# Windowed attention and a multiplicative feed-forward layer on one core: engine orders taken from a list schedule, row sums from added blocks, w_out loaded in halves

## The chip, the core and the metric

The kernel runs on one core of a Trainium2 chip. A core has five engines, each with an instruction stream of its own: TensorE (PE in the profile; PEld are its weight loads), VectorE (DVE), ScalarE (ACT), GpSimd (POOL) and SyncE (SP). They meet only through semaphores. Data lies in on-chip SBUF; TensorE writes its products to PSUM, a small accumulator memory. Loads and stores are DMA transfers issued by an engine's queue. Within an engine the instructions run in their written order, so an instruction that waits holds all that stand behind it.

The metric is the device time of one execution, in microseconds (us), as a median over runs.

## The reference

Attention over 4 batches, 8 heads, 768 positions and head size 64; a query sees the first four positions (the sinks) and the last 128. Its output goes, without a nonlinearity, through a feed-forward layer.

```python
    scores = scale * np.matmul(q, k.transpose(0, 1, 3, 2))
    keep = is_sink | in_window          # n_sink = 4, window = 128
    scores = np.where(keep, scores, -1000000000.0)
    a = np.exp(scores - max); a = a / (sum + 1e-09)
    attn = np.matmul(a, v)              # (4, 8, 768, 64)
    x = attn.transpose(0, 2, 1, 3).reshape(3072, 512)
    a = x @ w1                          # (512, 1024)
    b = x @ w2
    h = a * b @ w3                      # (1024, 1024)
    out = h @ w_out                     # (1024, 512)
```

Inputs are float32; the kernel casts them to bfloat16 in the loads and accumulates in float32.

## The kernel before, in words

**Fold.** As w3 and w_out are applied one after the other, the kernel first computes their product `w3o`. For each of the eight row blocks i of w3, `fold_w3(i)` transposes eight 128 x 128 blocks on TensorE (L249) and VectorE copies them out (L251); `fold_mm(i)` multiplies them by w_out in eight accumulating products of 512 columns (L257) and ScalarE copies the result to `w3o` (L259).

**Attention.** Per batch, k and q are transposed in three steps t of 256 positions (`transposes`, L154, copied by VectorE, L156). A unit is a pair of heads r (four) at a step t (three), so there are twelve a batch. `scores` computes the scores of a unit, keys on partitions (L191); ScalarE takes the exponential (L195, `ex`), VectorE multiplies by the mask (L198, `am`). At t = 0 there are three blocks of 128 x 128 per head, later four: for each of the two query blocks, the key block before it and its own, each masked to a triangle. `values` (L218) accumulates in one PSUM tile `av`, in column half 0 the products with v and in half 1 the row sums, which are products of the same `am` with a matrix of ones. The sinks have their own scores (`sink_scores`, L175, exponential L178) and values (`sink_values`, L163). ScalarE then forms the reciprocal of the sums as exp(-ln) (L223, L224), and VectorE multiplies (L225) into `xT`, the layer's input, transposed. The keys' and values' buffers are doubled or tripled over batches; `av` has one PSUM buffer, `sc` two, and all other products share three (`mm`).

**Layer.** `gate(b, c, dt)` makes one 128-row block dt of a and b for 384 tokens c of batch b: four products for `pa` (L233), a ScalarE copy (L236), four for `pb` (L239), and VectorE's multiplication (L241). There are 64 of these. `project(b, m)` makes 128 tokens of output from eight products of 512 columns (L265), a copy (L268) and a store by SP (L270). There are 24.

**What sets the order.** Loads are issued by GpSimd in one queue: w3's blocks 0 and 1, w_out, w3's blocks 2 to 4, then 5 to 7; after the selects that build masks, batch 0's k, q and v in blocks of 128 rows; w1 and w2 in halves; then the other batches. TensorE's order is written by hand: `attention(b)` steps through the units, and `fill(upto)` puts in the next piece of a list `dense` as a position advances through given spans. The list holds the fold, then each batch's gates and projections:

```python
    dense = [(0.6, fold_w3, (0,)), (0.6, fold_w3, (1,))]
    for i in range(KFF):
        if i + 2 < KFF:
            dense.append((0.45, fold_w3, (i + 2,)))
        dense.append((1.75, fold_mm, (i,)))
    ...
    spans = ((7.0, 17.6), (24.0, 49.2), (50.0, 80.0), (81.0, 110.0))
```

The transpose of w3 block 2 thus comes ahead of the first product with w_out, and batch 0's attention is spread over the rest of the fold. The framework orders ScalarE's and VectorE's instructions.

Of the kernel before, what the change touches and what calls it, by code (L numbers as in the profile page):

```python
# [21 lines left out]
def kernel(  # L22
# [81 lines left out]
    def load_w3(i0, n):  # L104
# [43 lines left out]
    def transposes(b, t):  # L148

        for src, dst in ((kN[b], kT[b]), (qN[b], qT[b])):  # L150
            tp = ps_mm.tile([P, NP, 2, P], BF16, tag="mm", name="tp")
            for r in range(NP):
                for i in range(2):
                    nc.tensor.transpose(tp[:, r, i, :], src[:, 2 * t + i, r * P:(r + 1) * P],  # L154
                                        ident[:])
            nc.vector.tensor_copy(dst[:, :, t * 256:(t + 1) * 256],  # L156
                                  tp[:].rearrange("p r i m -> p r (i m)"))

    def sink_values(b):

        vp = ps_mm.tile([P, H, D], FP32, tag="mm", name="vp")
        for h in range(H):
            nc.tensor.matmul(vp[:, h, :], sel[:, h, :], vN[b][:, 0, h * D:(h + 1) * D],  # L163
                             start=(h == 0), stop=(h == H - 1))
        nc.scalar.copy(vs[b][:], vp[:])
        for e in range(2):
            hp = slice(64 * e, 64 * e + 64)
            kk = ksbd[b][hp, 4 * e:4 * e + 640].rearrange("p (r x) -> p r x", x=160)
            nc.vector.tensor_copy(kk[:, :, 0:4], kT[b][hp, :, 0:4])

    def sink_scores(b, t):

        sp = ps_mm.tile([P, 256], FP32, tag="mm", name="sp")
        for r in range(NP):
            nc.tensor.matmul(sp[:], ksbd[b][:, r * P:(r + 1) * P],  # L175
                             qT[b][:, r, t * 256:(t + 1) * 256],
                             start=(r == 0), stop=(r == NP - 1))
        nc.scalar.activation(es[b][:, (t - 1) * 256:t * 256], sp[:], ACTF.Exp, scale=scale)  # L178


    def segments(t):
        segs = [] if t == 0 else [(2 * t - 1, 2 * t, P, 0)]
        return segs + [(2 * t, 2 * t, 2 * P, P), (2 * t + 1, 2 * t + 1, P, 3 * P)]

    def scores(b, r, t):
        c0 = P if t == 0 else 0
        sc = ps_sc.tile([P, 2, 512], FP32, tag="sc", name="sc")
        for i, (kb, qb, n, c) in enumerate(segments(t)):
            for e in range(2):
# [3 lines left out]
                                 start=True, stop=True)  # L193
        ex = work.tile([P, 2, 512], BF16, tag="ex", name="ex")
        nc.scalar.activation(ex[:, :, c0:], sc[:, :, c0:], ACTF.Exp, scale=scale)  # L195
        am = work.tile([P, 2, 512], BF16, tag="am", name="am")
        mk = maskt[:, min(t, 1):min(t, 1) + 1, c0:].to_broadcast([P, 2, 512 - c0])
        nc.vector.tensor_mul(am[:, :, c0:], ex[:, :, c0:], mk)  # L198
        return am

    def values(b, r, t, am):
# [3 lines left out]
        for kb, o, n, c in segs:  # L205
            for e in range(2):
                todo.append((e, 0, o, n, vN[b][:, kb, (2 * r + e) * D:(2 * r + e + 1) * D], am[:, e, c:c + n]))
            for e in range(2):
                todo.append((e, 1, o, n, ones[:], am[:, e, c:c + n]))
        if t > 0:  # L210
            sq = es[b][:, (t - 1) * 256:t * 256]
# [5 lines left out]
        for i, (e, y, o, n, lhs, rhs) in enumerate(todo):  # L217
# [3 lines left out]
            first[e] = False  # L221
        rec = work.tile([P, 256], FP32, tag="rec", name="rec")
        nc.scalar.activation(rec[:], av[:, 1, :], ACTF.Ln)  # L223
        nc.scalar.activation(rec[:], rec[:], ACTF.Exp, scale=-1.0)  # L224
        nc.vector.tensor_mul(xT[b][:, r, t * 256:(t + 1) * 256], av[:, 0, :], rec[:])  # L225

    def gate(b, c, dt):

        tk = slice(c * TOK, (c + 1) * TOK)
        d = slice(dt * P, (dt + 1) * P)  # L230
        pa = ps_mm.tile([P, TOK], FP32, tag="mm", name="pa")
        for kk in range(NP):
            nc.tensor.matmul(pa[:], w1_sb[:, kk, d], xT[b][:, kk, tk],  # L233
                             start=(kk == 0), stop=(kk == NP - 1))
        a_sb = work.tile([P, TOK], FP32, tag="a_sb", name="a_sb")
        nc.scalar.copy(a_sb[:], pa[:])  # L236
        pb = ps_mm.tile([P, TOK], FP32, tag="mm", name="pb")
        for kk in range(NP):
# [116 lines left out]
```

## Time and profile before

| what | us |
|---|---|
| median of three runs | 244.03 (243.27 to 245.24) |
| the profiled execution | 243.1 |
| its span, first to last instruction | 241.4 |
| TensorE busy | 214.9 |
| ScalarE busy | 132.7 |
| VectorE busy | 111.7 |

The profile is of one execution. Its page gives each engine's busy time, the span in 40 slices of about 6 us, the chain of work that ended last, and the costliest groups of instructions. The views of the trace behind it list instructions in order of time (the start, the duration, engine, line and operation, in brackets the idle time before it and what ended that), groups by shape, and who waited for whom. Matmuls are pipelined and their ends are modelled: successive ones overlap in these rows, so what a task takes of TensorE is read from one start to the next.

### The profile page before, as it was taken

The page shows a single profiled execution, that of the slowest core. Times are in us where ns is not written, and L with a number is a line of the kernel's source. Part 1 is how long each engine was busy: PE and PEld are TensorE (multiplying, and loading weights), DVE is VectorE, ACT ScalarE, POOL GpSimd, SP SyncE. Part 2 cuts the span into 40 slices and gives each one's busy share as a digit, 9 for nine tenths or more (in the row PEclk, how much of TensorE's full clock was granted, in tenths as well). Part 3 has the DMA queues.
Part 4 walks back from the last instruction along what each step waited for, and adds up shares of the span by engine and source line. Part 5 has one row for each costly group of instructions (what it writes and reads, how often), then busy time and mean ns, then how long its engine had stood idle before and what let it go on. Part 6 is the DMA issues. An engine that isn't in the chain of part 4 may idle for free.

```text
span 241.4 us, 4863 instructions
## 1 busy us (share of the span) xinstructions
PE 214.9 (89%) x1984; PEld 123.0 (51%) x1984; DVE 111.7 (46%) x211; ACT 132.7 (55%) x253; POOL 73.3 (30%) x90
## 2 busy tenths in 40 slices
PE   0329979687999999979999999999999999999994
PEld 0224656344656564446656654465565544566541
DVE  7202666542467664315656653157575531234300
ACT  2001576775365877744577777546766775333231
POOL 8946985499998098000000000000000000000000
PEclk9999999999999999999999999999999999999999
DMA  5999999999999999921000002220000022200033
GB/s 82 179 212 165 157 166 208 177 157 155 155 156 155 66 72 168 153 81 52 3 0 1 4 0 90 94 82 0 3 0 3 0 82 95 87 1 3 0 130 130
DMA packets 82582, 21.28 MB, mean 88 GB/s; under 512 B 75392, under 2 KB 78464, under 8 KB 82560
## 3 DMA queue, kind: packets, MB, share of 16 engines
q0 software_dynamic: 79104, 14.69, 74.5%
q1 hardware_dynamic: 3456, 6.29, 7.0%
q8 instruction: 15, 0.25, 0.4%
q14 instruction: 7, 0.06, 0.1%
HBM read 29.36 MB, written 6.29 MB: 148 GB/s over the span
## 4 chain that ended last, share of the span: by engine, by line
PE 85%; DMA 5%; ACT 4%; DVE 3%; issue 1%; POOL 1%; ACTq 0%; POOLq 0%
PE pa L233 19%; PE po L265 18%; PE pb L239 17%; PE av L218 13%; PE pw L257 7%; DMA w_sb<-in_moe_w_dram 5%; PE sc L191 5%; PE tp L154 4%; PE sp L175 1%; DVE xT_106 L225 1%; ACT rec L224 1%; ACT rec L223 1%; ACT ex L195 1%; ACT w3o L259 1%; DVE kT_102 L156 1%
## 5 line engine op out<-in xcount | busy, mean ns | idle before, releaser
L195 ACT ACTIVATE ex<-sc 128x1024 bf16<-128x1024 f32 (+1 forms) x48 | 45.3, 947 | 14.6 <-PE sc L191 14.6
L198 DVE TENSOR_TENSOR am<-ex,maskt 128x1024 bf16<-128x1024 bf16 (+1 forms) x48 | 31.1, 647 | 25.9 <-ACT ex L195 25.6
L236 ACT COPY a_sb<-pa 128x384 f32<-128x384 f32 x64 | 30.6, 478 | 21.9 <-DVE ab_113 L241 9.8
L239 PEld LDWEIGHTS <-w_sb 128*128 128x128 bf16 x256 | 25.0, 98 | 16.6
L233 PEld LDWEIGHTS <-w_sb 128*128 128x128 bf16 x256 | 21.8, 98 | 16.5 <-issue 4.3
L223 ACT ACTIVATE rec<-av 128x256 f32<-128x256 f32 x48 | 18.4, 383 | 16.5 <-PE av L218 16.3
L268 ACT COPY o_sb<-po 128x512 f32<-128x512 f32 x24 | 14.1, 586 | 20.8 <-PE po L265 20.8
L218 PE MATMUL av<-am,ones 128*64 128x128 bf16 (+1 forms) x256 | 24.1, 239 | 0.0
L224 ACT ACTIVATE rec<-rec 128x256 f32<-128x256 f32 x48 | 20.0, 417 | 1.5
L259 ACT CAST w3o<-pw 128x512 bf16<-128x512 f32 x8 | 4.7, 586 | 25.9 <-PE pw L257 25.9
L257 PE MATMUL pw<-wo_sb,w3t 128*128 128x512 bf16 x64 | 16.2, 399 | 0.5 <-ACT w3o L259 0.5
L241 DVE TENSOR_TENSOR ab_113<-a_sb,pb 128x384 bf16<-128x384 f32 x16 | 8.9, 555 | 14.8 <-PE pb L239 14.8
L218 PEld LDWEIGHTS <-ones 128*64 128x64 bf16 x256 | 14.8, 109 | 0.0
L233 PE MATMUL pa<-xT_108,w_sb 128*128 128x384 bf16 x64 | 13.2, 328 | 0.0
L233 PE MATMUL pa<-xT_107,w_sb 128*128 128x384 bf16 x64 | 13.1, 328 | 0.0
L233 PE MATMUL pa<-xT_106,w_sb 128*128 128x384 bf16 x64 | 13.1, 328 | 0.0
L239 PE MATMUL pb<-xT_108,w_sb 128*128 128x384 bf16 x64 | 13.0, 326 | 0.0
L239 PE MATMUL pb<-xT_107,w_sb 128*128 128x384 bf16 x64 | 13.0, 326 | 0.0
L239 PE MATMUL pb<-xT_106,w_sb 128*128 128x384 bf16 x64 | 13.0, 326 | 0.0
L233 PE MATMUL pa<-xT_109,w_sb 128*128 128x384 bf16 x64 | 13.0, 326 | 0.0
L239 PE MATMUL pb<-xT_109,w_sb 128*128 128x384 bf16 x64 | 13.0, 326 | 0.0
L249 PEld LDWEIGHTS <-w_sb 128*128 128x128 bf16 x64 | 4.8, 115 | 15.4 <-DMA w_sb<-in_moe_w_dram 14.7
(147 smaller groups left out, 361.3 us busy)
## 6 DMA issues: line engine op xcount, KB each, us to landing
out_dram<-o_sb SPq DMA_DIRECT2D x24, 256.0 KB, 2.0
w_sb<-in_moe_w_dram POOLq DMA_DIRECT2D x5, 512.0 KB, 10.5
w_sb<-in_moe_w_dram POOLq DMA_DIRECT2D x2, 768.0 KB, 14.7
wo_sb<-in_moe_w_out_dram POOLq DMA_DIRECT2D x1, 1024.0 KB, 10.4
kN_90<-in_k_dram POOLq DMA_DIRECT2D x6, 128.0 KB, 8.5
qN_86<-in_q_dram POOLq DMA_DIRECT2D x6, 128.0 KB, 7.1
vN_94<-in_v_dram POOLq DMA_DIRECT2D x6, 128.0 KB, 7.0
kN_91<-in_k_dram POOLq DMA_DIRECT2D x6, 128.0 KB, 7.3
```

Of the source, the lines that this page charges most:

```text
L191: nc.tensor.matmul(sc[:, e, c:c + n], kT[b][hp, r, kb * P:(kb + 1) * P], qT[b][hp, r, qb * P:qb * P + n], start=True, stop=True)
L195: nc.scalar.activation(ex[:, :, c0:], sc[:, :, c0:], ACTF.Exp, scale=scale)
L198: nc.vector.tensor_mul(am[:, :, c0:], ex[:, :, c0:], mk)
L218: nc.tensor.matmul(av[64 * e:64 * e + 64, y, o:o + n], lhs, rhs, start=first[e], stop=(i >= len(todo) - 2), skip_group_check=True)
L223: nc.scalar.activation(rec[:], av[:, 1, :], ACTF.Ln)
L224: nc.scalar.activation(rec[:], rec[:], ACTF.Exp, scale=-1.0)
L233: nc.tensor.matmul(pa[:], w1_sb[:, kk, d], xT[b][:, kk, tk], start=(kk == 0), stop=(kk == NP - 1))
L236: nc.scalar.copy(a_sb[:], pa[:])
L239: nc.tensor.matmul(pb[:], w2_sb[:, kk, d], xT[b][:, kk, tk], start=(kk == 0), stop=(kk == NP - 1))
L257: nc.tensor.matmul(po[:], w3T[i][:, j, :], wo_sb[:, j, :], start=(j == 0), stop=(j == KFF - 1))
L265: nc.tensor.matmul(po[:], ab[b][:, kk, m * P:(m + 1) * P], w3o[:, kk, :], start=(kk == 0), stop=(kk == KFF - 1))
L268: nc.scalar.copy(o_sb[:], po[:])
```

## The change: what it does

It has three parts.

1. *Loads.* w3 comes in blocks 0; 1; 2 and 3; 4 and 5; 6 and 7, and w_out in two halves of its columns, the first behind w3's block 0, the second behind block 3. `fold_mm` is split by the same halves: sixteen tasks of eight products of 256 columns. The transposed block of w3 has five buffers for two.
2. *Row sums.* For t > 0 VectorE adds, for each query block, its two masked key blocks into a tile `cs` (256 columns a head); as their masks are complementary triangles, the values are the window's terms at each place of the query, folded onto 128 partitions. The product with ones then runs once, over `cs`.
3. *Order.* Each piece of work becomes a task with stages on TensorE, ScalarE or VectorE, written as a Python generator that yields after each stage. Tasks have a priority, tasks that must be done or started before, loads they need and a PSUM ring. While the program is built, a list scheduler plays the stages through with written durations, modelled landing times and handovers of 0.2 us, and issues the instructions in the order in which that model starts them, on all three engines. A gate is two tasks, one for each half.

The core of the diff:

```diff
     nc.scalar.preload_act_table_set("natural_log_exp_and_others")
-    load_w3(0, 2)
-    load_w(wo_sb, moe_w_out, 0, DM)
-    load_w3(2, 3)
-    load_w3(5, 3)
     nc.vector.memset(ident[:], 1.0)
+    load_w3(0, 1)
     nc.gpsimd.affine_select(ident[:], ident[:], compare_op=ALU.is_equal, fill=0.0,
                             base=0, pattern=[[1, P]], channel_multiplier=-1)
+    load_w(wo_sb, moe_w_out, 0, DM // 2)
+    load_w3(1, 1)
+    load_w3(2, 2)
+    load_w(wo_sb, moe_w_out, DM // 2, DM)
+    load_w3(4, 2)
+    load_w3(6, 2)
...
-        am = work.tile([P, 2, 512], BF16, tag="am", name="am")
+        yield
+        am = work.tile([P, 2, 512], BF16, tag="am", bufs=4, name="am")
         mk = maskt[:, min(t, 1):min(t, 1) + 1, c0:].to_broadcast([P, 2, 512 - c0])
         nc.vector.tensor_mul(am[:, :, c0:], ex[:, :, c0:], mk)
+        cs = None
+        if t > 0:
+            cs = work.tile([P, 2, 256], BF16, tag="cs", bufs=4, name="cs")
+            a4 = am[:].rearrange("p e (a c q) -> p (e a) c q", c=2, q=P)
+            nc.vector.tensor_add(cs[:].rearrange("p e (a q) -> p (e a) q", q=P),
+                                 a4[:, :, 0, :], a4[:, :, 1, :])
+        ams[b, r, t] = am, cs
+        yield
...
             for e in range(2):
-                todo.append((e, 1, o, n, ones[:], am[:, e, c:c + n]))
+                if t == 0:
+                    todo.append((e, 1, o, n, ones[:], am[:, e, c:c + n]))
         if t > 0:
+            for e in range(2):
+                todo.append((e, 1, 0, 256, ones[:], cs[:, e, :]))
...
+    def gate(b, c, dt, half):
         tk = slice(c * TOK, (c + 1) * TOK)
+        w_sb = w2_sb if half else w1_sb
+        pg = ps_mm.tile([P, TOK], FP32, tag="mm", name="pg")
         for kk in range(NP):
+            nc.tensor.matmul(pg[:], w_sb[:, kk, dt * P:(dt + 1) * P], xT[b][:, kk, tk],
                              start=(kk == 0), stop=(kk == NP - 1))
+        yield
+        if half:
+            nc.vector.tensor_mul(ab[b][:, dt, tk], gate_a.pop((b, c, dt))[:], pg[:])
+        else:
+            a_sb = work.tile([P, TOK], FP32, tag="a_sb", bufs=4, name="a_sb")
+            nc.scalar.copy(a_sb[:], pg[:])
+            gate_a[b, c, dt] = a_sb
+        yield
...
+    def fold_mm(i, n):
+        po = ps_mm.tile([P, DM // 2], FP32, tag="mm", name="pw")
+        cols = slice(n * DM // 2, (n + 1) * DM // 2)
         for j in range(KFF):
+            nc.tensor.matmul(po[:], w3T[i][:, j, :], wo_sb[:, j, cols],
                              start=(j == 0), stop=(j == KFF - 1))
+        yield
+        nc.scalar.copy(w3o[:, i, cols], po[:])
+        yield
...
+    for i in range(KFF):
+        task(("t3", i), 100 + i, fold_w3(i), [("pe", 0.5), ("dve", 0.65)], loads=[("w3", i)],
+             started=[("fm", i - 5, 1)] if i > 4 else [], ring="mm")
+        for n in range(2):
+            task(("fm", i, n), 100.5 + i + 3 * n, fold_mm(i, n), [("pe", 0.9), ("act", 0.42)],
+                 [("t3", i)], [("wo", n)], "mm")
...
+                task(("sc", b, r, t), 4, scores(b, r, t),
+                     [("pe", 0.27), ("act", 0.83), ("dve", 0.58)] if t == 0 else
+                     [("pe", 0.36), ("act", 1.05), ("dve", 1.05)], after, ring="sc",
...
+                task(("av", b, r, t), 3, values(b, r, t),
+                     [("pe", 0.42 if t == 0 else 0.68), ("act", 0.85), ("dve", 0.45)],
...
+                task(("g", b, c, dt, 0), pr + 0.5, gate(b, c, dt, 0), [("pe", 0.66), ("act", 0.5)],
+                     [("av", b, NP - 1, last_t)] + war, [("w1", n), ("w2", n)], "mm",
+                     [("g",) + gates[-2] + (1,)] if len(gates) > 1 else [])
+                task(("g", b, c, dt, 1), pr, gate(b, c, dt, 1), [("pe", 0.66), ("dve", 0.56)],
+                     [("g", b, c, dt, 0)], ring="mm", half=True)
...
+    HOP = 0.2
+    MARGIN = {"av": 0.5}
+    BACKLOG = 1.6
+    free = {"pe": 0.0, "act": 0.0, "dve": 0.0}
+    rings = {n: [[0.0] for _ in range(k)] for n, k in (("mm", 3), ("sc", 2), ("av", 1))}
...
+    def pe_pick():
...
+            est = max([free["pe"]] + [arrive[x] + HOP for x in k["loads"]])
+            if not k["half"]:
+                est = max([est] + [done[a] + HOP for a in k["after"]])
+            if k["ring"]:
+                if rings[k["ring"]][0][0] is None:
+                    continue
+                est = max(est, rings[k["ring"]][0][0] + HOP)
+            if est > free["pe"]:
+                est += MARGIN.get(kind, 0.0)
+            if kind == "sc":
+                busy = max(0.0, free["act"] - free["pe"]) + sum(q[2] for q in queue["act"])
+                est = max(est, free["pe"] + busy - BACKLOG)
+            wait = est - free["pe"]
+            key = (0.0 if wait < 0.05 else wait, k["prio"])
...
+    with tc.manual_schedule(engines={mybir.EngineType.PE, mybir.EngineType.Activation,
+                                     mybir.EngineType.DVE}):
+        while len(done) < len(tasks):
+            pe = pe_pick()
+            moves = [(pe[2], 0, "pe")] if pe else []
+            for e in ("act", "dve"):
+                at = [when(q) for q in queue[e] if when(q) is not None]
+                if at:
+                    moves.append((max(free[e], min(at)), 1, e))
+            start, _, e = min(moves)
```

A lower number is a higher priority: transposes 1, sink work 2, values 3, scores 4, the fold 100 to 111, gates of batch b from 1000 + 200 b, its projections from 1300 + 200 b. The first two steps of a batch's attention open the gates of its first 384 tokens, the third those of its last 384; before, all of a batch's gates came behind its attention.

More of the change, by code (lines that the diff above doesn't have):

```diff
@@ new lines, in when, with advance @@
+    def when(q):
+        at, _, _, k = q
+        if k["half"]:
+            return max(at, done[k["after"][0]] + HOP) if k["after"][0] in done else None
+        return at
+    def advance(k, at):
+        i = k["stage"]
+        if k["ring"] and i == {"mm": 1, "sc": 1, "av": 2}[k["ring"]]:
+            k["cell"][0] = at
+        k["stage"] = i + 1
+        if i + 1 < len(k["stages"]):
+            e, us = k["stages"][i + 1]
+            queue[e].append((at + HOP, k["prio"], us, k))
+        else:
+            done[k["name"]] = at
```

196 lines of the change are left out of this document (124 added, 72 removed).

## The prediction, made before the changed kernel ran

> **What bounds the kernel now.** I read the page first, then the timeline of the head, the chain that ended last, the groups by shape, and the waits.
>
> ```profile
> span 241.4 us, 4863 instructions
> PE 214.9 (89%) x1984; PEld 123.0 (51%) x1984; DVE 111.7 (46%) x211; ACT 132.7 (55%) x253; POOL 73.3 (30%) x90
> PE   0329979687999999979999999999999999999994
> PE 85%; DMA 5%; ACT 4%; DVE 3%; issue 1%; POOL 1%; ACTq 0%; POOLq 0%
> ```
>
> TensorE carries 85% of the chain and is full from the tenth slice on; no other engine passes 55%. Its holes lie in the first quarter. The timeline of the head shows the first kind:
>
> ```profile
> 3.03 1.51 POOL L105 DMA_DIRECT2D w_sb<-in_moe_w_dram  x2
> 6.74 1.04 PE L249 MATMUL tp_226<-ident,w_sb 128*128 128x128 bf16 x8 [6.74 <-DMA w_sb<-in_moe_w_dram]
> 7.57 1.06 PE L249 MATMUL tp_237<-ident,w_sb 128*128 128x128 bf16 x8
> 16.30 1.03 PE L249 MATMUL tp_248<-ident,w_sb 128*128 128x128 bf16 x8 [7.67 <-DMA w_sb<-in_moe_w_dram]
> 17.12 2.94 PE L257 MATMUL pw<-wo_sb,w3t 128*128 128x512 bf16 x8
> 27.62 1.51 ACT L195 ACTIVATE ex<-sc 128x768 bf16<-128x768 f32 x2 [0.30 <-PE sc L191]
> ```
>
> Up to 16.30 TensorE has transposed two w3 blocks; it then waits 7.67 us for the third, because the written order puts that transpose ahead of the first fold product. The first exponential of batch 0 starts at 27.62. The chain shows where batch 0's attention ends, and the tail:
>
> ```profile
> 58.30 0.78 PE av L218 x16
> 59.09 0.76 PE pa L233 x4
> 59.84 0.65 PE pb L239 x4
> 60.49 0.65 PE pa L233 x4
> 227.43 10.37 PE po L265 x48
> ```
>
> The first gate runs at 59.09, behind all of the fold and all of batch 0's attention. TensorE ends at 227.43 + 10.37 = 237.8; the last copy and store take 3.6 us to 241.4.
>
> **TensorE's own price of each task**, from starts of consecutive rows while it is full (durations in these rows overlap):
>
> ```profile
> 112.53 0.40 PE L163 MATMUL vp<-vN_96,sel 128*128 128x64 bf16 x8
> 112.77 0.81 PE L233 MATMUL pa<-xT_107,w_sb 128*128 128x384 bf16 x4
> 118.72 0.61 PE L154 MATMUL tp<-ident,kN_92 128*128 128x128 bf16 x8
> 119.17 0.61 PE L154 MATMUL tp<-ident,qN_88 128*128 128x128 bf16 x8
> 121.39 0.30 PE L218 MATMUL av<-am,vN_96 128*64 128x256 bf16 x2
> 121.52 0.28 PE L218 MATMUL av<-am,ones 128*64 128x256 bf16 x2
> 121.63 0.22 PE L218 MATMUL av<-am,vN_96 128*64 128x128 bf16 x2
> 121.68 0.22 PE L218 MATMUL av<-am,ones 128*64 128x128 bf16 x2
> 121.84 0.61 PE L175 MATMUL sp<-qT_100,ksbd_116 128*128 128x256 bf16 x4
> 122.38 0.34 PE L191 MATMUL sc<-qT_100,kT_104 64*128 64x256 bf16 x4
> 122.65 0.82 PE L233 MATMUL pa<-xT_107,w_sb 128*128 128x384 bf16 x4
> 125.92 0.40 PE L191 MATMUL sc<-qT_100,kT_104 64*128 64x128 bf16 x6
> 126.25 0.82 PE L233 MATMUL pa<-xT_107,w_sb 128*128 128x384 bf16 x4
> ```
>
> Sink values 0.24, a transpose task 0.45, a values unit 0.45 at t = 0 and 0.78 later (58.30 to 59.09), sink scores 0.54, scores 0.27 and 0.33, a half gate 0.65, a 512-wide product of eight 10.37/6 = 1.73. Batch 0 and the fold, which end at 59.09: fold 8 x (0.45 + 1.73) = 17.4, transposes 6 x 0.45 = 2.7, sinks 0.24 + 1.08, scores 4 x 0.27 + 8 x 0.33 = 3.7, values 4 x 0.45 + 8 x 0.78 = 8.0: 33.1 us of work in 59.1 us. What follows: the three other batches' attention, 3 x 15.7 = 47.1; gates 128 x 0.65 = 83.2; projections 24 x 1.73 = 41.5; together 171.8 in 178.7 us (59.1 to 237.8). So 6.9 us go between tasks over three quarters of the run, and 26 us in the first quarter. That quarter is where something is to be had.
>
> **The change, part by part.**
>
> *Row sums.* In 32 units (t > 0) the sums' pairs of 128, 256 and 128 columns become one pair of 256. Of the rows at 121.4 a pair of 256 takes 0.11 and a pair of 128 about 0.05: 0.78 - 0.10 = 0.68, so 24 units after batch 0 give -2.4 us. The price is one VectorE addition of 512 results per unit.
>
> ```profile
> L198 DVE TENSOR_TENSOR am<-ex,maskt 128x1024 bf16<-128x1024 bf16 x32 | 22.1, 692 | 18.0 <-ACT ex L195 17.9
> L198 DVE TENSOR_TENSOR am<-ex,maskt 128x768 bf16<-128x768 bf16 x16 | 8.9, 558 | 7.9 <-ACT ex L195 7.8
> L195 ACT ACTIVATE ex<-sc 128x1024 bf16<-128x1024 f32 x32 | 32.5, 1016 | 6.5 <-PE sc L191 6.5
> L195 ACT ACTIVATE ex<-sc 128x768 bf16<-128x768 f32 x16 | 12.8, 809 | 8.0 <-PE sc L191 8.0
> L224 ACT ACTIVATE rec<-rec 128x256 f32<-128x256 f32 x48 | 20.0, 417 | 1.5
> L223 ACT ACTIVATE rec<-av 128x256 f32<-128x256 f32 x48 | 18.4, 383 | 16.5 <-PE av L218 16.3
> L225 DVE TENSOR_TENSOR xT_106<-av,rec 128x256 bf16<-128x256 f32 x12 | 5.1, 424 | 8.4 <-ACT rec L224 7.8 <-PE sc L191 0.6
> ```
>
> 256 elements more cost 134 ns, so 512 cost about 692 - 268 = 0.42; the upper bound, with split runs at the full row, is 0.69. That is 13 to 22 us more on an engine with 241 - 112 us to spare. It lies on the path from exponential to values, which has two other units to cover it; without that cover it would be 32 x 0.42 = 13 us. I take nothing.
>
> *w3 and w_out in seven loads for four.* Bytes are the same, and k and q of batch 0 queue behind them as before, so I keep 27.62 for the first exponential. Fold products can run from about 8 us on; TensorE may do some 14 of the fold's 18 us before that attention starts, against about 7 before. Halving w_out's columns makes 16 products of 256 columns: between 0.87 (half of 1.73) and 1.07 (twice 0.54); I take 0.92, nearer the same operation. Half a microsecond in all, in idle time.
>
> GpSimd issues three loads more, at about 0.75 each (1.51 for the two at 3.03), so its mask selects and the first k load come some 2.3 us later. The cover is its own queue, which next stands still for a landing:
>
> ```profile
> 16.54 0.88 POOL L98 DMA_DIRECT2D kN_90<-in_k_dram  x1 [2.82 <-DMA w_sb<-in_moe_w_dram]
> ```
>
> Without that cover the 2.3 us would reach batch 0's k and q; SP's stores are not touched.
>
> *List schedule.* Fold, attention and gates are now taken by readiness. Gates of batch 0's first 384 tokens need only t = 0 and 1, eight units, not twelve, and no longer stand behind the rest of the fold. What paces those units is the single values buffer: product, Ln 0.38, Exp 0.42, multiply 0.42, then the next product. With about 0.2 for handovers that is 1.9 us (0.45 at t = 0) and 2.1 us (0.68 later). ScalarE's own load, 0.38 + 0.42 + 1.02 = 1.82 us per later unit, just fits. The first values follow the first exponential by 0.81 + 0.56 + 0.3, at 29.3; eight units give 29.3 + 4 x 1.9 + 4 x 2.1 = 45.3. I add 0.7 for fold copies and exponentials of t = 2 in ScalarE's queue: 46. (Scores of batches 2 and 3 are made to wait for the gates two batches back, whose xT they overwrite; TensorE has other gates then, so I cost it at nothing.) Ends: 43 without the handovers, 50 if ScalarE's work for later units always goes first.
>
> By 46 TensorE has done fold 8 x 0.45 + 16 x 0.92 = 18.3, transposes 2.7, sinks 0.8, scores 3, values 4 x 0.45 + 4 x 0.68 = 4.5: 29.3 us. The whole job is now 33.1 + 171.8 - 32 x 0.10 + 0.9 = 202.6, so 173.3 remain. With the 6.9 us between tasks kept, TensorE ends at 46 + 173.3 + 6.9 = 226.2 and the span at 229.8.
>
> *ScalarE and VectorE orders fixed.* Neither is added to. A late producer now holds all that stands behind it on its engine: a gate copy behind a values unit's Ln, and behind the copy one of three shared PSUM buffers that TensorE needs. Bounds: -3 us (fewer crossings) to the rival below; I take 0.
>
> Sum: span 241.4 - 11.6 = 229.8. The profiled execution took 243.1, 1.7 over its span, so 231.5; the median of the runs, 244.03, is 0.9 above that execution. I say 231.5.
>
> **Rivals.**
>
> *A, fixed orders stall TensorE (slower).* Each half gate holds one of three buffers until a copy or multiply that can't overtake an exponential of 1.02. If it loses 0.13 us on each of 128 halves, that is +16.6: 248. It decides from 11.6/128 = 0.09 us on. Against it stand TensorE's waits now:
>
> ```profile
> PE tp_248 L249 <- DMA w_sb<-in_moe_w_dram: 7.7, 1, 7.7
> PE tp_226 L249 <- DMA w_sb<-in_moe_w_dram: 6.7, 1, 6.7
> PE av L218 <- DVE xT_106 L225: 6.1, 7, 1.4
> ```
>
> None is for the gates' buffers, though there are three of them now too. For it: durations written into the plan are guesses, and VectorE's 0.42 is not measured.
>
> *B, more loads land later.* Issue to landing:
>
> ```profile
> DMA to landing us min/median/max: 5.4/13.2/16.2
> ```
>
> The first w3 load (two blocks) landed 5.4 after its issue; the second and third (three blocks each, issued 0.73 apart) 3.0 + 0.73 = 3.7 apart, 1.25 a block. So the first carries 5.4 - 2.5 = 2.9 beyond its bytes. If three more loads each paid that one after another, all behind them shifts by 8.7: 240.2. Against it: the back-to-back pair shows no such part. The Trainium skill, in "DMA: Bandwidth & Descriptors" (Anatomy of one DMA; Bandwidth), gives a fixed cost of about 2.0 us per transfer and advises 1 MiB or more; paid serially that would make an estimate of 6 us and 237.5. By that rule the split is a loss; the pair of rows speaks for hiding it.
>
> *C, the plan packs better.* Gates at 43 and half of the 6.9 lost: 231.5 - 3 - 3.4 = 225. For it: pure stretches (59.84 to 60.49 is 0.65) lose nothing, and attention goes first, so more of the end is pure.
>
> **How the numbers follow.** Forecast 0.55; C 0.15; B 0.12; A 0.18, of which 0.12 is its full form and 0.06 a weaker one that only eats the gain. About 1% is what a measurement of this kernel tells from no change (241.6 to 246.5). Forecast, C and 0.08 of B are faster: 0.78; 0.04 of B and 0.06 of A the same: 0.10; slower 0.12. The range runs from C's 225, less 1, to B's 240 and a little more: 224 to 241.
>
> **What would show it.** Products of the fold before 12 us and no wait near 7.7; first gate at 43 to 50, not 59; a values unit at 0.68; TensorE's end near 226; the addition at about 0.42. A first exponential much after 27.6 would be B. Waits of TensorE for gate copies or multiplies summing over 8 us would be A and make the forecast wrong; a gate start near 59 would say the plan does not bring batch 0 forward.

## The result, and the profile after

The changed kernel takes 237.49 us (median of four runs, 234.89 to 238.05) against 243.97 (243.27 to 245.24): a ratio of 0.9708, 95% interval 0.9626 to 0.9789. It is faster, by 6.5 us where the prediction said 12.5, and lies inside the stated range. The profiled execution took 237.69 with a span of 236.0; the sum had said 229.8 for the span, so 6.2 us of the forecast gain are missing. In this document medians are over all executions of a kernel, while ratios and intervals leave out the executions in the chip's slower state (one each of e1, e3 and e5) and are against executions of the kernel before taken along with that run, whose medians were 243.30 to 244.13.

The page of the changed kernel, the same four lines as before and the granted clock:

```profile
span 236.0 us, 4744 instructions
PE 215.4 (91%) x1920; PEld 130.2 (55%) x1920; DVE 120.7 (51%) x243; ACT 134.8 (57%) x261; POOL 75.2 (32%) x93
...
PE   1389996579999999999999999999999999999993
...
PEclk9999999956999999999999999999999999999999
...
PE 85%; DMA 4%; DVE 4%; ACT 3%; POOL 1%; issue 1%; POOLq 0%; ACTq 0%
```

From the tenth slice on TensorE is full; before it was from the eleventh. The holes are still in the first quarter, but have moved: the wait near 12 us is smaller, a new thin place stands at 35 to 53 us (the seventh to the ninth slice), and the granted clock falls to half from 46.4 us on, which the profile of the kernel before does not show.

The timeline of the changed kernel, TensorE's rows of the head, of batch 0's values at t = 1 and of the end, with ScalarE's first exponential among them:

```profile
5.25 1.04 PE L285 MATMUL tp_229<-ident,w_sb 128*128 128x128 bf16 x8 [5.25 <-DMA w_sb<-in_moe_w_dram]
10.25 1.86 PE L297 MATMUL pw<-wo_sb,w3t 128*128 128x256 bf16 x8 [3.96 <-DMA wo_sb<-in_moe_w_out_dram]
...
29.86 0.61 PE L156 MATMUL tp<-ident,kN_90 128*128 128x128 bf16 x8
...
32.98 2.23 ACT L211 ACTIVATE ex<-sc 128x768 bf16<-128x768 f32 x3
...
44.52 0.41 PE L248 MATMUL av<-am,vN_94 128*64 128x128 bf16 x6 [1.06 <-DVE xT_106 L257]
...
46.64 0.64 PE L248 MATMUL av<-am,vN_94 128*64 128x128 bf16 x6 [1.05 <-DVE xT_106 L257]
...
49.30 0.64 PE L248 MATMUL av<-am,vN_94 128*64 128x128 bf16 x6 [0.84 <-DVE xT_106 L257]
...
57.34 2.12 PE L268 MATMUL pg<-xT_106,w_sb 128*128 128x384 bf16 x12
...
227.68 4.70 PE L307 MATMUL po<-w3o,ab_113 128*128 128x512 bf16 x21
```

Fold products start at 10.25, as intended. But batch 0's transposes come at 29.86, where they came at 25.02 before, its first exponential at 32.98 for 27.62, and the first gate at 57.34, not at 46.

The clock, stage by stage (us and count of instructions for each engine, then granted clock, DMA share and GB/s):

```profile
39.60:43.00 3.40, 1.96 (x32) 1.33 (x27) 3.25 (x6) 2.04 (x5) 1.43 (x2) 1.00 1.24 206
43.00:46.40 3.40, 1.53 (x30) 1.02 (x25) 2.20 (x5) 2.89 (x7) 1.19 (x2) 1.00 1.53 193
46.40:49.80 3.40, 2.31 (x26) 1.68 (x27) 1.79 (x5) 2.36 (x4) 2.27 (x3) 0.50 2.39 155
49.80:53.20 3.40, 2.56 (x29) 1.54 (x27) 2.25 (x5) 1.71 (x3) 3.16 (x5) 0.50 2.43 157
53.20:56.60 3.40, 3.40 (x38) 2.44 (x38) 2.29 (x5) 2.37 (x5) 3.40 (x5) 0.50 2.42 156
```

At 43 to 46.4 TensorE is busy 1.53 of 3.40 us; then it runs at half clock for 10.2 us, and the step from one values unit to the next goes from 44.52 to 46.64 (2.12) to 46.64 to 49.30 (2.66).

The groups by shape show the new prices:

```profile
L221 DVE TENSOR_TENSOR cs<-am 128x512 bf16<-128x512 bf16 x32 | 13.6, 425 | 1.1
L297 PE MATMUL pw<-wo_sb,w3t 128*128 128x256 bf16 x128 | 18.2, 300 | 4.0 <-DMA wo_sb<-in_moe_w_out_dram 4.0
```

### The profile page after: what moved, and what is told of

It is laid out like the page before. It is cut to its first block, busy times and chain, and to the rows that moved or that the text cites. A ratio compares the mean times of both kernels' runs of the same rounds, so it can differ in the third digit from the quotient of the medians.

```text
span 236.0 us, 4744 instructions
## 1 busy us (share of the span) xinstructions
PE 215.4 (91%) x1920; PEld 130.2 (55%) x1920; DVE 120.7 (51%) x243; ACT 134.8 (57%) x261; POOL 75.2 (32%) x93
## 4 chain that ended last, share of the span: by engine, by line
PE 85%; DMA 4%; DVE 4%; ACT 3%; POOL 1%; issue 1%; POOLq 0%; ACTq 0%
PE pg L268 37%; PE po L307 18%; PE av L248 13%; PE pw L297 6%; PE sc L206 5%; DMA w_sb<-in_moe_w_dram 4%; PE tp L156 3%; PE sp L186 2%; ACT ex L211 1%; ACT rec L254 1%; DVE xT_106 L257 1%; DVE am L215 1%; ACT rec L255 1%; DVE kT_105 L159 1%; DVE qT_101 L159 1%
## 5 line engine op out<-in xcount | busy, mean ns | idle before, releaser
L268 PEld LDWEIGHTS <-w_sb 128*128 128x128 bf16 x512 | 47.7, 98 | 33.2 <-issue 4.5
L275 ACT COPY a_sb<-pg 128x384 f32<-128x384 f32 x64 | 30.7, 479 | 29.3 <-PE pg L268 15.4
L211 ACT ACTIVATE ex<-sc 128x1024 bf16<-128x1024 f32 (+1 forms) x48 | 44.8, 937 | 1.1 <-PE sc L206 1.1
L215 DVE TENSOR_TENSOR am<-ex,maskt 128x1024 bf16<-128x1024 bf16 (+1 forms) x48 | 30.8, 642 | 8.7 <-ACT ex L211 8.6
L254 ACT ACTIVATE rec<-av 128x256 f32<-128x256 f32 x48 | 18.4, 384 | 14.3 <-PE av L248 13.2
L268 PE MATMUL pg<-xT_106,w_sb 128*128 128x384 bf16 x128 | 23.8, 327 | 0.1
L268 PE MATMUL pg<-xT_108,w_sb 128*128 128x384 bf16 x128 | 22.4, 327 | 0.0
L268 PE MATMUL pg<-xT_107,w_sb 128*128 128x384 bf16 x128 | 22.4, 327 | 0.0
L297 PE MATMUL pw<-wo_sb,w3t 128*128 128x256 bf16 x128 | 18.2, 300 | 4.0 <-DMA wo_sb<-in_moe_w_out_dram 4.0
L268 PE MATMUL pg<-xT_109,w_sb 128*128 128x384 bf16 x128 | 21.0, 326 | 0.0
L300 ACT CAST w3o<-pw 128x256 bf16<-128x256 f32 x16 | 6.0, 372 | 24.9 <-PE pw L297 24.9
L297 PEld LDWEIGHTS <-w3t 128*128 128x128 bf16 x128 | 13.3, 107 | 6.5 <-issue 3.2
L272 DVE TENSOR_TENSOR ab_113<-a_sb,pg 128x384 bf16<-128x384 f32 x16 | 8.8, 553 | 13.1 <-PE pg L268 13.1
L272 DVE TENSOR_TENSOR ab_111<-a_sb,pg 128x384 bf16<-128x384 f32 x16 | 8.8, 552 | 10.9 <-PE pg L268 10.9
L221 DVE TENSOR_TENSOR cs<-am 128x512 bf16<-128x512 bf16 x32 | 13.6, 425 | 1.1
L272 DVE TENSOR_TENSOR ab_112<-a_sb,pg 128x384 bf16<-128x384 f32 x16 | 8.8, 551 | 10.2 <-PE pg L268 10.2
L272 DVE TENSOR_TENSOR ab_110<-a_sb,pg 128x384 bf16<-128x384 f32 x16 | 8.8, 550 | 5.1 <-PE pg L268 5.0
L307 PE MATMUL po<-w3o,ab_110 128*128 128x512 bf16 x48 | 11.4, 380 | 0.0
L307 PE MATMUL po<-w3o,ab_111 128*128 128x512 bf16 x48 | 11.0, 380 | 0.0
L307 PE MATMUL po<-w3o,ab_112 128*128 128x512 bf16 x48 | 10.7, 379 | 0.0
## 6 DMA issues: line engine op xcount, KB each, us to landing
w_sb<-in_moe_w_dram POOLq DMA_DIRECT2D x7, 512.0 KB, 11.3
```

Source lines behind the costliest of these rows:

```text
L221: nc.vector.tensor_add(cs[:].rearrange("p e (a q) -> p (e a) q", q=P), a4[:, :, 0, :], a4[:, :, 1, :])
L268: nc.tensor.matmul(pg[:], w_sb[:, kk, dt * P:(dt + 1) * P], xT[b][:, kk, tk], start=(kk == 0), stop=(kk == NP - 1))
L272: nc.vector.tensor_mul(ab[b][:, dt, tk], gate_a.pop((b, c, dt))[:], pg[:])
L275: nc.scalar.copy(a_sb[:], pg[:])
L297: nc.tensor.matmul(po[:], w3T[i][:, j, :], wo_sb[:, j, cols], start=(j == 0), stop=(j == KFF - 1))
L307: nc.tensor.matmul(po[:], ab[b][:, kk, m * P:(m + 1) * P], w3o[:, kk, :], start=(kk == 0), stop=(kk == KFF - 1))
```

## The experiments

All are variants of the changed kernel unless it is said otherwise. The table has, beside each time, three instants of its profile: the first exponential of batch 0, the first gate, and how long TensorE takes from the first gate to the end of its last matmul; and how long the granted clock stood at half.

| kernel | median us | ratio to before (95%) | first exp. | half clock | first gate | gate to end |
|---|---|---|---|---|---|---|
| before | 243.97 | | 27.6 | 0 | 59.0 | 178.8 |
| changed | 237.49 | 0.9708 (0.9626 to 0.9789) | 33.0 | 10.2 | 57.3 | 175.0 |
| e1, loads of before | 238.64 | 0.9764 (0.9683 to 0.9845) | 35.3 | 10.2 | 59.7 | 175.1 |
| e2, other plan | 238.08 | 0.9761 (0.9708 to 0.9814) | 28.3 | 10.2 | 57.9 | 174.2 |
| e3, busy head | 236.95 | 0.9667 (0.9579 to 0.9756) | 30.5 | 17.1 | 56.5 | 175.1 |
| e4, batch 0's scores x3 | 235.49 | 0.9657 (0.9599 to 0.9715) | 30.8 | 0 | 53.9 | 175.0 |
| e11, batch 2's scores x3 | 240.14 | 0.9869 (0.9835 to 0.9903) | 31.9 | 3.4 | 55.3 | 179.7 |
| e6, TensorE's order alone | 236.66 | 0.9647 (0.9583 to 0.9710) | 32.4 | 10.2 | 56.3 | 175.3 |
| e5, before + row sums | 242.48 | 0.9897 (0.9840 to 0.9954) | 28.8 | 0 | 60.7 | 176.1 |
| e12, without row sums | 239.56 | 0.9835 (0.9794 to 0.9876) | 30.4 | 10.2 | 52.7 | 180.4 |
| e7, e2 in part + e4 | 236.03 | 0.9657 (0.9593 to 0.9720) | 29.0 | 0 | 53.4 | 177.0 |
| e8, k, q, v first | 232.02 | 0.9480 (0.9437 to 0.9523) | 11.5 | 6.8 | 49.8 | 176.9 |
| e9, e8 + busy head | 231.35 | 0.9519 (0.9481 to 0.9558) | 12.0 | 0 | 49.7 | 176.1 |
| e10, e9, TensorE's order alone | 232.18 | 0.9541 (0.9491 to 0.9591) | 12.3 | 0 | 49.3 | 177.1 |

The last column is the first reading: with the changed order it hardly moves (174 to 177) unless work is added or taken away (e11, e12). A kernel's span is its first gate plus some 176 us plus 3.6. So most questions below are what sets the first gate.

**e1: the loads of before.**

```diff
-    load_w3(0, 1)
+    load_w3(0, 2)
+    load_w(wo_sb, moe_w_out, 0, DM)
+    load_w3(2, 3)
+    load_w3(5, 3)
...
-    load_w(wo_sb, moe_w_out, 0, DM // 2)
-    load_w3(1, 1)
-    load_w3(2, 2)
-    load_w(wo_sb, moe_w_out, DM // 2, DM)
-    load_w3(4, 2)
-    load_w3(6, 2)
```

> The changed kernel with the loads of before (w3 blocks 0-1, all of w_out, blocks 2-4, blocks 5-7); orders as in the changed kernel. Theory L (the seven loads make batch 0 late): the last w3 block lands at 20.0 us instead of 21.8, so does everything queued behind it, the first exponential comes 1.8 earlier than 32.98, and the time falls from 237.5 to about 235.7. Rival P (the written order holds batch 0's transposes behind fold products, and those are late because TensorE ran slowly and waited before 19 us): the first product waits for all of w_out until 12.5 and the third block until 16.3, so TensorE comes to the transposes as late as before or 1 to 2 us later, and the time is 237.5 to 239.

Measured: first exponential 35.3, 2.3 later than in the changed kernel; 238.64. Rival P's account came true in the trace: the first product waited until 12.55, and the transposes came later, not earlier. The time is less clear: the trace is of an execution at 240.09, two others took 237.2, and by the intervals the two kernels cannot be told apart. The split loads are not what made batch 0 late; in the traces they bring it forward.

**e2: the plan's numbers.**

```diff
-    for i in range(KFF):
-        lands(("w3", i), wblk)
...
+    for i, us in enumerate((5.2, 11.5, 14.0, 14.0, 19.3, 19.3, 21.8, 21.8)):
+        arrive["w3", i] = us
+    arrive["wo", 0], arrive["wo", 1] = 10.2, 16.7
...
-                us = k["stages"][0][1]
+                us = k["stages"][0][1] * (2.0 if start < 19.1 else 1.0)
```

> The changed kernel with other numbers in the plan alone: landing times as measured in the changed kernel's trace (w3 5.2, 11.5, 14.0, 19.3, 21.8, halves of w_out 10.2 and 16.7, then 0.85 per k, q or v block and 2.54 per half of w1 or w2), and TensorE stages twice as long before 19.1 us. Same work; the plan now puts batch 0's transposes ahead of eight more fold products. Theory P: first exponential near 28.5 instead of 32.98, fold products fill TensorE's gaps between 33 and 45, no drop of the granted clock near 46, first gate 4 to 6 us earlier than 57.3, time 232 to 234. Rival V (the single values buffer paces batch 0 however it is ordered): the first exponential is earlier, but units then take longer, and the time stays within 1 us of 237.5.

Measured: the first exponential came at 28.3, 4.7 earlier; the time did not fall (238.08). Theory P was right about the late start and wrong that it was the price: the first gate came at 57.9, no earlier than in the changed kernel. Of TensorE's waits in this kernel, one is new:

```profile
PE vp L176 <- DMA vN<-in_v_dram: 4.0, 2, 3.4
```

The plan had batch 1's sink values ahead of batch 0's remaining values units; TensorE reached them early and stood 3.4 us for a load, with those units behind it. And the clock halved all the same, from about 44.2 us. Neither theory had named that wait.

**e3: products that nothing reads, in the head.**

```diff
+    def warm(n):
+        wt = ps_mm.tile([P, P], FP32, tag="mm", name="wt")
+        for _ in range(n):
+            nc.tensor.matmul(wt[:], ident[:], ident[:], start=True, stop=True)
...
+        if i == 0:
+            warm(28)
...
+        if i == 0 and n == 0:
+            warm(48)
```

> The changed kernel with 28 products of 128 columns of the identity with itself ahead of the first w3 transpose and 48 more ahead of the first fold product, into a PSUM tile that nothing reads; all else as in the changed kernel. Theory W (TensorE's half speed up to 19.1 us makes it late for the transposes): the granted clock is full from about 9 us, a fold half takes 0.87 instead of 1.66 at 17 us, transposes of batch 0 begin near 27.0 instead of 29.86, and the time falls by 2 to 3 us. Rival L (landings make it late): the clock is full early, but TensorE waits for blocks that land at 14.0, 19.3 and 21.8; transposes begin no more than 1 us earlier, time within 1 us of 237.5.

Measured: TensorE's products had their full-clock price from 5.3 us on (a group of w3's transposes 0.45 for 0.85), batch 0's transposes began at 27.3 and the first exponential 2.5 earlier, as Theory W said. But TensorE had less left to do later on (1.63 of 3.40 us busy from 36 us), the granted clock was at half from 39.4 to 56.4, and the first gate came only 0.8 earlier; 236.95 is not told from the changed kernel.

**e4 and its control e11: scores issued three times,** in batch 0 (e4, below) or in batch 2 (e11).

```diff
-        for i, (kb, qb, n, c) in enumerate(segments(t)):
+        for i, (kb, qb, n, c) in enumerate(segments(t) * (3 if b == 0 else 1)):
```

> The changed kernel with the score products of batch 0 issued three times over (the last time counts), 8 us more of TensorE's work where it idles. Theory C (TensorE's idleness at 40 to 50 us halves its granted clock from 46.4 to 56.7, and that costs time): the clock stays full, a values unit of batch 0 takes 0.67 instead of 1.21 at 47 us, the first gate comes 2 us earlier, time 235 to 236. Rival V (the values buffer's chain through ScalarE and VectorE paces it, the clock is hidden): clock full, but the time is unchanged or up to 2 us longer.

> Control to e4: the changed kernel with the score products of batch 2 instead of batch 0 issued three times over, the same 8 us of extra work where TensorE is full. Theory C (e4 gained from the clock in batch 0's idle stretch): the clock halves near 46 us for 10 us as in the changed kernel, and the time is 237.5 + 6 to 8 = 243.5 to 245.5. Rival (repeated scores help in themselves, by spacing the values units): the time is under 240.

Measured in e4: the clock stayed full, with more work on TensorE. Its stages:

```profile
43.00:46.40 3.40, 2.79 (x60) 2.20 (x59) 2.32 (x5) 2.69 (x6) 1.50 (x2) 1.00 1.49 194
46.40:49.80 3.40, 2.18 (x47) 1.73 (x42) 2.31 (x5) 3.04 (x5) 1.76 (x3) 1.00 2.38 156
```

and its timeline, the step of a values unit again and the first gate:

```profile
45.10 0.41 PE L248 MATMUL av<-am,vN 128*64 128x128 bf16 x6 [0.61 <-DVE xT L257]
...
47.22 0.41 PE L248 MATMUL av<-am,vN 128*64 128x128 bf16 x6 [0.61 <-DVE xT L257]
...
53.94 2.12 PE L268 MATMUL pg<-xT,w_sb 128*128 128x384 bf16 x12
```

The step stays 2.12, and the first gate is 3.4 us earlier. Not all of that is the halved clock: the first exponential was already 2.2 earlier, with the same head program, because the products happened to reach their full-clock price before 13.8 us and not at about 19. From the first exponential to the first gate it is 23.2 against 24.4, so the halved clock at 46 us cost about 1.2 us in this pair of traces, 1.08 of it in the two steps between units that took 2.66. The intervals of the two times overlap; the trace carries this, not the medians. In e11 extra work of the same kind costs: gate to end is 179.7, 4.6 more than in the changed kernel, and the time is 240.14, between what the two theories said. Theory C's other half did not come: its clock was at half for 3.4 us only, from 51.9, though nothing in batch 0 had been changed. Its first gate was 2.0 earlier, which takes part of the price back. So repeated scores are free in batch 0's thin stretch and paid for where TensorE is full.

**e6: ScalarE and VectorE ordered by the framework.**

```diff
-    with tc.manual_schedule(engines={mybir.EngineType.PE, mybir.EngineType.Activation,
-                                     mybir.EngineType.DVE}):
+    with tc.manual_schedule(engines={mybir.EngineType.PE}):
```

> The changed kernel with TensorE's order alone fixed; ScalarE's and VectorE's instructions are ordered by the framework as in the kernel before. Theory (the fixed orders of the two engines cost nothing that matters; the loss lies in batch 0): time within 1.5 us of 237.5, same first gate near 57. Rival A (a late producer holds what stands behind it on these engines): 3 us or more faster. Rival (the fixed orders are what helps): 3 us or more slower.

Measured: 236.66, within 1 us; gate to end 175.3. Fixing these two orders neither cost nor gave anything that could be told.

**e5 and e12: the row sums alone, and all but the row sums.** e5 adds `cs` and its products with ones to the kernel before; e12 takes them out of the changed one.

> The kernel before with the row sums alone: VectorE's addition and one pair of products with ones in place of three, loads and orders as before. Theory S (TensorE is full behind the first quarter, so 0.10 us a unit is had 24 times): values units at 0.68, time 244.1 - 2.4 = 241.7. Rival (the longer path exponential, mask, addition, values makes TensorE wait in its fixed order): units at 0.68 but gaps ahead of them, time 243.5 or more.

> The changed kernel without the added blocks: three pairs of products with ones per unit as before, no additions on VectorE, and the plan's stage times to match (values 0.78, mask 0.70). Theory S (TensorE is full behind the first quarter, 0.10 to 0.11 us a unit): 24 to 32 units, time 2.4 to 3.4 us over the changed kernel, 240 to 241. Rival (the additions cost what they save, by way of later values): within 1 us of 237.5.

Measured: e5 242.48, ratio 0.9897 (1.1 to 3.9 us by its interval), and gate to end 176.1 for 178.8: the 2.4 us of the prediction, within what can be told. e12 is 2.1 over the changed kernel with an interval just clear of it. Its gate to end is 5.4 longer, more than 32 x 0.10, and its first gate 4.7 earlier: 2.6 by an earlier first exponential, the rest, by the traces, because its order has eight values units ahead of the first gate where the changed kernel has nine (the last ones start at 49.43 and at 55.10), so more of batch 0 was left for later. So e12 is not the sums alone. The two directions agree on 2 to 3 us.

**e7: an earlier start and a held clock together.** The plan of e2 for w3, w_out and the half speed before 19.1 us, with the changed kernel's own landing times from batch 0's k on, and e4's repeated scores.

> Two edits together: the plan has the measured landings of w3 and w_out and TensorE at half speed up to 19.1 us, but everything from batch 0's k on lands in the plan as in the changed kernel, so that batch 1's sink values are not put ahead of their landing; and batch 0's scores are issued three times over. Theory P+C (a late start of batch 0 and the halved clock each cost, and each edit alone left the other): first exponential near 29, clock full from 20 us on, first gate at 50 to 52, time 232 to 234. Rival V (the values buffer's chain makes the first gate late whatever comes before): first gate at 54 or later and time 235 or more.

Measured: first exponential 29.0, granted clock full throughout, yet the first gate at 53.4 and 236.03: the rival's time, with a first gate between what the two said. With both faults mended batch 0 still needs 24.4 us from its first exponential to the first gate; fold products and repeated scores now stand between the units. What paces this stretch is the units themselves and what the order puts between them.

**e8 to e10: batch 0's k, q and v first.** If that stretch cannot be made much shorter, it can be begun earlier. `load_kqv` loads single blocks; the mask selects stand between these loads, the rest follows as before. The plan's landing times match, and it takes TensorE's work as twice as long before 12 us.

```diff
+    load_kqv(0, 0, "k")
...
+    load_kqv(0, 0, "q")
+    load_kqv(0, 1, "kq")
...
+    load_kqv(0, 0, "v")
+    load_w3(0, 1)
+    load_kqv(0, 1, "v")
...
+    load_w(wo_sb, moe_w_out, 0, DM // 2)
+    load_w3(1, 1)
+    load_w3(2, 2)
+    for kb in (2, 3):
+        load_kqv(0, kb)
+    load_w(wo_sb, moe_w_out, DM // 2, DM)
+    load_w3(4, 2)
+    load_w3(6, 2)
+    for kb in (4, 5):
+        load_kqv(0, kb)
```

> The changed kernel with the first quarter loaded in another order: batch 0's first two blocks of k, q and v ahead of everything, then half of w3 and w_out, blocks 3 and 4 of k, q and v, the other half, the last two blocks; w1 and w2 after that as before. The plan is given landing times to match (estimates from the spacing 0.85 and 2.5 of the traces). Theory H (the loss is the head: attention of batch 0 cannot start before 27 us while TensorE waits): first exponential near 11, the fold fills TensorE between its units, batch 0 and the fold done by 44 when w1 and w2 land, first gate near 43, time 222 to 226. Rival (TensorE is now too sparsely used up to 40 us and its clock stays at half, or loads in small pieces land later): first gate near 50, time 230 to 235.

Measured: 232.02, ratio 0.9480 (0.9437 to 0.9523), faster than both kernels. The first exponential came at 11.5, the first gate at 49.8, not 43: on time and gate the rival's numbers came. (The plan in this kernel itself has the first gate at 49.5.) Its stage of half clock:

```profile
13.70:17.10 3.40, 1.32 (x20) 1.01 (x17) 2.20 (x5) 2.50 (x6) 3.40 (x5) 1.00 1.24 166
17.10:20.50 3.40, 2.96 (x22) 1.80 (x20) 0.69 (x1) 0.37 (x1) 2.41 (x3) 0.50 1.26 179
```

e9 asks whether that was the reason. Besides the edits below, its plan has the landing times of e8's trace.

```diff
+        if src is kN[0] and t == 0:
+            warm(24)
...
+        if b == 0:
+            warm(10)
...
+        if (i, n) == (0, 0):
+            warm(16)
...
-        for i, (kb, qb, n, c) in enumerate(segments(t)):
+        for i, (kb, qb, n, c) in enumerate(segments(t) * (3 if b == 0 and t == 0 else 1)):
```

> e8 (batch 0's first k, q and v loaded ahead) with two edits: the plan has the landings that e8's trace shows, and TensorE gets products that nothing reads where it waits before 19 us (24 ahead of the first transpose, 10 ahead of the sink values, 16 ahead of the first fold product; batch 0's first four score units three times over). Theory C (e8 lost TensorE's clock from 17.1 to 23.9, at 7 us of half speed): clock full from 13 us at the latest and kept, first gate 2 to 3 us ahead of 49.84, time 228 to 230.5. Rival (that stretch waits for w_out's first half at 16.7 and w3 at 18.6 and 21.2 anyway): clock full, first gate within 1 us of 49.84, time 231 to 232.5.

> e9 with TensorE's order alone fixed. Theory (e6: the two other engines' fixed orders cost a little under 1 us): 0 to 1.5 us under e9. Rival A (they cost several us where the plan is tight): 3 us or more under e9. Rival (they help): 1 us or more over e9.

Measured: e9's granted clock is never at half, its products have their full-clock price from 12.4 us at the latest, and its first gate is at 49.7, 231.35: the rival. It cannot be told from e8. e10, 232.18, was expected 0 to 1.5 us under e9 and came 0.8 over it, which cannot be told from no change. e9's stages show where time is left:

```profile
20.00:30.00 10.00, 7.47 (x87) 5.66 (x87) 4.71 (x10) 4.99 (x10) 6.19 (x8) 1.00 1.85 178
30.00:40.00 10.00, 10.00 (x133) 7.94 (x132) 7.06 (x14) 5.68 (x12) 6.15 (x9) 1.00 1.81 182
40.00:50.00 10.00, 10.00 (x122) 7.55 (x123) 6.40 (x14) 8.75 (x19) 3.41 (x4) 1.00 1.44 196
```

TensorE is full from 30 us on; what can still be had lies ahead of that, where it waits for loads (2.3 us in all for w_out, 2.1 for batch 0's k). How much of it a better order of the loads would bring was not tried.

## Why the prediction came out half right

The direction and the range held, the place of the gain did not. The forecast gain was to come from a first gate at 46 us for 59; the gate gave 1.7 us. The other 3.7 us of the shorter span lie behind the gate, and e5 shows some 2.6 there from the row sums alone.

*Row sums: right.* Sixteen matmuls became twelve; a unit takes 0.67 us of TensorE where 0.68 was said, the addition 425 ns where 0.42 was said, and e5's time agrees with the 2.4 us.

*Fold halves: right.* A half takes 0.87 us at full clock (24.81 to 27.43 for three), the lower of the two bounds.

*"I keep 27.62 for the first exponential": the step that failed.* The bytes ahead of batch 0's k and q were the same, and the last of w3 ahead of them did land only 1.8 us later. But the transposes stand in a fixed order behind thirteen fold halves. The plan has those done by 24.8 us; TensorE waited 4.0 us for w_out's first half, worked at about half its later pace up to some 19 us, and came to the transposes at 29.86:

```profile
14.83 1.91 PE L297 MATMUL pw<-wo_sb,w3t 128*128 128x256 bf16 x8
16.54 1.06 PE L285 MATMUL tp_281<-ident,w_sb 128*128 128x128 bf16 x8
...
24.81 2.78 PE L297 MATMUL pw<-wo_sb,w3t 128*128 128x256 bf16 x24
27.43 0.61 PE L285 MATMUL tp_415<-ident,w_sb 128*128 128x128 bf16 x8
```

A half takes 1.71 from 14.83 and 0.87 from 24.81. In e8, at a granted clock of 0.50, a half takes 1.68 (20.51 to 22.19), so this is the price of half the clock; the profile's granted clock reads 1.00 in this head all the same, and that it was a halved clock is inferred from the prices.

The prediction costed the fold's earlier start as work moved into idle time and did not ask what stands behind it. e2, which only moves the transposes up, brings the first exponential back to 28.3, and e3, which only mends the price of the products, to 30.5. The late start is 5.4 of the 11.3 us by which the first gate is late. That mending it would have brought the gate forward is not shown: e2 brings it back and leaves the gate at 57.9, with its new wait of 3.4 us on the way.

*The pace of the values units: mis-sized.* 18.4 us from first exponential to first gate were said; 24.4 were measured. The eight steps from the first values to the ninth unit took 20.3 (34.84 to 55.10), where 4 x 1.9 + 4 x 2.1 = 16.0 were said. About 1.2 of the difference is the halved clock (e4: 23.2). The rest, by the traces, is in what the order puts between: in e4, and in the changed kernel too, the fourth unit came 3.4 after the third, its order behind sink scores that wait for a copy of transposed q, and behind the eighth unit batch 1's transposes and another unit come before the first gate. The prediction reckoned 1.9 and 2.1 for a unit with nothing in between; 2.12 is right only where nothing is.

The order was not made with those rates either, and the kernel says so before any run. Its plan has a later unit every 0.68 + 0.85 + 0.45, three handovers of 0.2 and the margin of 0.5: 3.08 us. Worked through with its own numbers, it puts the first gate at 55.3 us, behind nine units and batch 1's first transposes, not at 46 behind eight. The trace's 57.3 is 2.1 from that. The other plans, worked through, have the first gate at 58.0 in e2 (57.9 measured), 56.4 in e7 (53.4) and 49.5 in e8 (49.8). No run changes the plan's unit times, so it is not shown how far shorter ones would bring the gate forward.

*The clock: not in the prediction at all.* It took full-clock prices throughout, as the kernel before had from 19 us on. Before, fold products lay between batch 0's units up to 58 us, and TensorE was busy 24.67 of the 31 us from 28 to 59; in the changed kernel it was busy 5.61 of the ten from 40 to 50. Bringing the fold forward removed that filler; e4 and e7, with other products in its place, kept the clock. What the halved clock costs is not settled: beside the 1.2 us of e4 stand e1's executions, with spans of 235.4 and 235.5 at a mean granted clock of 1.0 and of 238.4 at 0.979, and what else differed between them is not on record.

*Given back later: 5.2 us.* Gate to end was said to be 180.2 (46 to 226.2) and is 175.0: by the late first gate more attention work is done. 11.3 less 5.2 is 6.1 of the missing 6.2.

*Rivals.* A, fixed orders of ScalarE and VectorE, is excluded as a large cost by e6; a TensorE order fixed against modelled times does cost, as the late transposes and e2's 3.4 us wait show. B said that a late first exponential would point to the loads; e1 shows that reading wrong. The last block of w3 landed 1.8 us later (21.8 for 20.0), far from 8.7. The 237.5 of B's smaller estimate is the measured time by chance: it rested on landings 6 us later. C did not come. One reading of the view before was a slice off: TensorE was full there from the eleventh slice, not from the tenth.

## What to carry to other kernels

A fixed order is only as good as the times that it was planned with: work the plan through to the instant that is forecast before reckoning with rates of your own, and then look in the trace for the first instruction that the engine reaches later, or earlier, than the plan had it, and for what stands behind it. Work moved forward into a hole leaves a hole where it was; ask what that work was covering there. When the stretch that sets the end is a chain of small handovers, starting it earlier can give more (e8: 5 us here) than polishing what surrounds it.

## What the runs showed of the hardware that was not expected

TensorE's granted clock falls to half without any long pause. In the changed kernel no wait between 39.6 and 46.4 us is over 1.5 us, yet the clock halved behind a stretch of 3.4 us that was busy 1.53 (45%). In e3 the stretch was:

```profile
36.00:39.40 3.40, 1.63 (x27) 1.19 (x24) 2.62 (x5) 2.85 (x5) 2.54 (x3) 1.00 1.28 206
39.40:42.80 3.40, 2.38 (x20) 1.36 (x21) 1.90 (x5) 1.74 (x4) 1.36 (x2) 0.50 1.24 206
```

48% there, 39% in e8 (13.7 to 17.1). How busy the last 3.4 us were does not decide it alone. In e11 three such stretches in a row were busy 53 to 54% and the clock fell only behind the third:

```profile
41.61:45.02 3.41, 1.82 (x32) 1.28 (x33) 2.22 (x5) 2.89 (x7) 0.96 (x2) 1.00 1.24 206
45.02:48.44 3.42, 1.85 (x34) 1.33 (x35) 2.32 (x5) 2.65 (x6) 1.77 (x3) 1.00 2.24 161
48.44:51.85 3.41, 1.84 (x35) 1.21 (x32) 2.73 (x6) 2.97 (x6) 2.53 (x3) 1.00 2.42 157
51.85:55.27 3.42, 3.42 (x33) 2.29 (x32) 2.14 (x4) 1.71 (x4) 3.27 (x4) 0.50 2.43 157
```

The kernel before kept its full clock through these, and cut at another instant one of them is far emptier:

```profile
46.50:49.90 3.40, 2.05 (x33) 1.30 (x32) 1.81 (x3) 2.85 (x7) 3.30 (x4) 1.00 2.43 154
49.90:53.40 3.50, 2.44 (x31) 1.25 (x29) 1.54 (x3) 2.85 (x6) 3.26 (x5) 1.00 2.43 155
53.40:56.80 3.40, 2.02 (x34) 1.44 (x34) 1.12 (x2) 1.49 (x4) 3.40 (x5) 1.00 2.43 156
...
52.40:55.80 3.40, 1.03 (x22) 0.83 (x23) 1.54 (x3) 2.16 (x5) 3.40 (x5) 1.00 2.43 157
```

59% to 70%, but 30% from 52.4. Where such stretches should be cut is not on record for this kernel, so no edge can be read from these rows. The stretches at half were 3.4, 6.8, 10.2 and 17.1 us long, whole multiples of 3.4. In the changed kernel the last 3.4 us at half were busy throughout (53.2 to 56.6), and the 3.4 before them, busy 2.56, did not end it. The Trainium skill, in "TensorE: Matmul & The Clock Gate" (Part 1), gives a free-running window of about 3.4 us, which these lengths agree with, and has the clock fall after an idle window; here stretches busy for 39 to 54% were enough.

What one such stretch goes with can be read from the kernel before. Of its 21 executions taken along with the experiments, five have a mean granted clock of 0.993 and spans of 243.6 to 243.9, the others 0.999 or more and 241.4 to 242.5. Over 243.7 us, 0.007 below full is 3.4 us at half, an estimate from these means; it goes with about 2 us.

The instant at which TensorE's products first reach their full-clock price is not the program's alone. Kernels with the same head as the changed one had it between 12.4 and 13.8 us (e4, e12) and at about 19 (the changed kernel), and their first exponential moved with it, from 30.4 to 33.0. A difference of 2 us between two profiles of such a kernel can be no more than that.
